# Four heads' last 64 queries in one block: joint remainder scoring in an attention and gated MLP kernel

## The chip, the cores and the metric

The kernel runs on one core of a Trainium2 chip. The core has a matrix engine (TensorE, PE in the profile), a vector engine (VectorE, DVE), a scalar engine (ScalarE, ACT), a general engine (GpSimd, POOL) and a queue engine (SyncE, SP) that issues nearly all transfers. The metric is the time of one execution in microseconds, the median of several runs. The profile describes one execution.

## The reference

Eight batches, eight heads, 576 positions, 64 values per head. Attention with a bias that depends on the position of the query and on the distance to the key, and then a gated layer: a causal convolution with five taps gives the gate, and one matrix product before and one after it mix the 512 channels.

```python
scores = scale * np.matmul(q, k.transpose(0, 1, 3, 2))
x = (psi_rel / psi_i)[..., None]            # log1p|i-j| / log1p(max(i,1))
bias = np.maximum(x @ w1 + b1, 0.0) @ w2    # one value per head
scores = scores + bias.transpose(2, 0, 1)[None, :, :, :]
attn = softmax(scores)                      # written out in the reference
x = matmul(attn, v), heads side by side     # (8, 576, 512)
gate = sigmoid(causal 5-tap convolution of x by conv_w)
out = (gate * (x @ w_val)) @ w_out
```

Everything is float32.

## The kernel before

**Pairs.** The work of attention is cut into 32 pairs of heads: `pair(n)` handles heads 2p and 2p+1 of batch b, where `order` lists the pairs so that two pairs with l = 0 and l = 1 of the same batch and the same half of the heads follow each other. One pair's queries and keys lie in one tile `qk`, head 0 on partitions 0 to 63 and head 1 on partitions 64 to 127, since a head has 64 values.

**Blocks.** The 576 queries of a head make four blocks of 128 (c = 0 to 3) and a remainder of 64 (c = 4, `NM`). For a main block `qkm` (L623) scores both heads with four matmuls: two halves of 288 keys for each head. The 64-row contractions of the two heads occupy different row halves of PE. Each f32 matmul shows as two records in the trace. For the remainder `qkr` (L635) the host has laid out the last 64 queries of both heads in one 128x128 stationary matrix and the keys of both heads in 640 columns with zeros between (`QW`, `RW`), so that two matmuls of 320 columns over all 128 rows give 64 rows of scores for each head. The part of the 640 columns that belongs to no key of the row is masked through the bias tile `biasr`, which holds -1e30 there.

**After the scores.** `logits` (L665, DVE) adds the bias and takes the maximum, `expo` (L677, ACT) exponentiates and sums. Then there are two ways, chosen for each pair in `TRANS`. A "T" pair is normalised in float32 (`norm`, L722, POOL or DVE), transposed on PE with an identity (`tp`, L762), copied out of PSUM (`tev`, ACT or DVE) and multiplied with V in float32. A "D" pair is split into two float16 halves (`top`, then `rest`, L252, mostly POOL), transposed by a DMA on SP's queue (`swap`, L796, for a main block and L799 for the remainder), and multiplied in three float16 products; the sums are divided out at the end through a small product with the identity (`rb`, L881; in the remainder L914) and a multiplication (`mu`, `mur`). `piece` (L832) is the product with V for two blocks at a time, in two column halves of PE, one per head; `rem_mm` (L904) is that of the remainder.

**The gated layer.** When all four pairs of a batch are done, `mlp` runs its convolution on DVE, and the products `val` (L1075) and `outp` (L1132) on PE. Before all attention, `bias_rows` builds the bias for all heads in DRAM (L365 on PE), from which `load_bias` fetches 128 queries of two heads at a time.

**Order.** `Plan` holds every step as a task with the engines that may run it, an estimated cost, its dependencies, a priority and the buffers that it takes. `Plan.order` walks through the tasks with a model of the engines, takes on each engine the ready task with the best priority, picks the engine for tasks that may run on several (weighted by `LOAD`), and thus writes out a fixed order for each engine; the chip then executes these queues in order. The priorities come from tables: `PAIR_AT` for each pair, `MLP_AT` for each batch, `OFFS` for each kind of step. `BUFS` gives the number of buffers in each ring, `RING` the ring that each kind of buffer uses, `LOOK` how far a ring may be taken out of order, and `MODES` the tiling of PE for each kind of step, whose change the model charges.

Of the kernel before, what the change touches and what calls it, by code (L numbers as in the profile page):

```python
# [32 lines left out]
NEG = -1.0e30  # L33
RW = S + REM
QW = (NM + 1) * P
# [6 lines left out]
MLP_AT = (27, 17, 14, 9, 8, 19, 12, 70)  # L42
PAIR_AT = (1, 3, -1, 0, -0.5, -1, 2.5, -2.5, -4.5, -5, -0.5, -0.5, -0.5, 0.5, 2.5, -1.5, -2, -2.5, -2, 1.5, 1.5, 1, -2.5, -0.5, -1.5, -5, -5.5, -7, 0, 3, 0.5, 0.5)
TRANS = tuple(x == "T" for x in "TTTDTTTTDTTDDTDDDDDTDDTDDDDDDDDD")
BUFS = dict(w=13, d=5, pt=2, sp=2, ps=4, qk=2, rel=4, be=6, xp=2, xh=1, gh=1, gx=1)
RING = dict(er="w", hlr="w", raw="w", e="d", hl="d", xo="w", vt="w", ptr="w", gate="w", gf="w", ot="w", tt="ps", po="ps", pm="ps", cv="ps")
LOOK = dict(w=14.02, ps=60.04, d=6.72, be=3.8, gh=227.3, pt=9.76, xh=21.35, sp=1.22, xp=0.44)
# [9 lines left out]
OFFS = dict(qkr=-5, ldx=3, swap=4.25, qk_ld=-1, qkm=-5, norm=4, piece=4, val=5.25, outp=7.75, mur=2.25, bias_store=-0.75, conv=-9.25, taps=-5.25, split_hi=-0.25, rb=-4.5, rest=-15.5, ldv=0.5, w_hi=-1, logits=1.75, relu=-3.25, ost=-1.25, bias_fin=0.25, ote=0.25, double_step=10.5, store=1, ghi=1.75, sig=-5.75, vtr=5, recip=-3, glo=-1, ev=3.25, tev=4, evr=1, w_sub=-7.5, gf=-3, w_ld=-5.25, mu=0, w_lo=7.5, bias_mm=0, bias_ld=0.75, expo=-2.25, prod=-1.25, vlo=1, cw=-3, vhi=5, eps=-0.25, vmax=-15.5, acc=0, split_lo=5.5, close_bias=2.5, rem_mm=4, top=-0.25, vinv=-0.25, tp=-3.25, vscale=-1.75, constant=4.75, constant_ev=-2)  # L57
# [147 lines left out]
def attention_gated_mlp(  # L205
# [23 lines left out]
    for k in set(BUFS) & {"sp", "ps", "w", "d", "pt", "qk"}:  # L229
        mem = dict(space=PSUM) if k in ("sp", "ps") else {}  # L230
        pools[k] = ctx.enter_context(tc.tile_pool(name="pool_" + k, bufs=1, **mem))
# [25 lines left out]
    biasr = [cp.tile([P, RW], F32, name=f"biasr_{l}") for l in range(2)]  # L257
# [55 lines left out]
    for t in biasr:  # L313
        G.memset(t[0:REM, S:RW], NEG)
        G.memset(t[REM:P, 0:REM], NEG)

# [113 lines left out]
    def load_bias(run, hg, l, c, pri):  # L430

        p = 2 * hg + l

        def bias_ld(e):
            if c < NM:
                SP.dma_start(biasm[l][c], bias_rows_of(c, 2 * p, 2))
            else:
                SP.dma_start(biasr[l][0:REM, 0:S], bias_rows_of(c, 2 * p, 1))
                SP.dma_start(biasr[l][REM:P, REM:RW], bias_rows_of(c, 2 * p + 1, 1))

        deps = stored[c] + users_of_bias.get((run - 1, l, c), [])
        return add([("S", 1.65 if c < NM else 0.9)], bias_ld, deps, pri)
# [87 lines left out]
    spilled, arrived, taker = {}, {}, {}  # L530

    def pair(n):
# [4 lines left out]
        tr = TRANS[n % len(TRANS)]  # L537
        pace = PACE[n] if n < len(PACE) else 2
        top_, bot = slice(0, D), slice(D, P)
# [3 lines left out]
        def qk_ld(e):  # L543
            SP.dma_start(new(qk, [P, QW + RW], F32), qkd[b, p])

        loaded = add([("S", 1.85)], qk_ld, (), s0 - 8, [qk])
# [59 lines left out]
        ptr = Buf("ptr")  # L606
        nms, rinvs, sm, invs, rsum = {}, {}, None, {}, {}
        es, exps, inv = {}, {}, {}
# [3 lines left out]
        for c in range(NM + 1):  # L612
            w = S if c < NM else RW
            sps = [Buf("sp") for _ in range(2 if c < NM else 1)]

            def qkm(e, c=c, sps=sps):
# [3 lines left out]
                for j in range(2):  # L620
                    for a, r in enumerate((top_, bot)):
                        x = QW + a * REM + j * hw
# [8 lines left out]
            def qkr(e, sps=sps):  # L631

                t, hw = new(sps[0], [P, 2, 512], F32), RW // 2
                for j in range(2):
                    T.matmul(  # L635
                        t[:, j, 0:hw],
                        lhsT=qk.t[:, NM * P : QW],
                        rhs=qk.t[:, QW + j * hw : QW + (j + 1) * hw],
                        start=True,
                        stop=True,  # L640
                    )

            qkt = add([("P", 1.17 if c < NM else 1.1)], qkm if c < NM else qkr, [loaded], s0 + pace * c, sps, [qk])
            for a in range(2 if c < NM else 1):
                h = s0 + pace * c + a
                sp = sps[a]
                if a == 0:
                    eb = Buf("e" if c < NM else "er")
                    es[c] = eb

                def part(c=c, a=a, w=w):
                    return es[c].t[:, a * S : a * S + w]

                def logits(e, c=c, a=a, w=w, sp=sp, part=part):
                    if a == 0:
                        new(es[c], [P, 2 * S if c < NM else RW], F32)
                    nonlocal sm
                    if a == 0:
                        nms[c] = smp.tile([P, 2], F32, name="nm", tag="nm", bufs=20)
# [4 lines left out]
                    bias = biasm[l][c][:, a, :] if c < NM else biasr[l]  # L664
                    V.tensor_tensor_reduce(  # L665
                        out=part().rearrange("p (j f) -> p j f", j=2),
                        in0=sp.t[:, :, 0 : w // 2],
# [8 lines left out]
                def expo(e, c=c, a=a, part=part):  # L676
                    A.activation(  # L677
                        out=part(),
                        in_=part(),
# [6 lines left out]
                def eps(e, c=c):  # L686

                    if tr:
                        rinvs[c] = smp.tile([P, 2], F32, name="rinv", tag="rinv", bufs=20)
                        o, u = rinvs[c], sums[c]  # L690
                        if c == NM:
                            o, u = o[:, 0:1], u[:, 0:1, :]
                    else:
                        x, w = (c // 2 * 4, 4) if c < NM else (8, 1)
# [11 lines left out]
                t1 = qkt  # L706
                bl = bias_task.get((run, l, c))
                if bl is None:
                    bl = bias_task[run, l, c] = load_bias(run, hg, l, c, h - 6)
                t2 = lg = add([("V", 0.68)], logits, [t1, bl, lg if a else None], h + 0.5, [eb] if a == 0 else (), [sp])  # L710
                users_of_bias.setdefault((run, l, c), []).append(t2)
                t3 = add([("A", 0.77)], expo, [t2], h + 1)
                exps[c, a] = t3
                if tr:
                    if c < NM and a == 0:
                        continue
                    tr_ = add([("V", 0.08)], eps, [exps[c, x] for x in range(a + 1)], h + 1.3)
                    tr_ = add([("V", 0.08)], recip, [tr_], h + 1.5)

                    def norm(e, a, c=c, w=w):  # L720
                        t = es[c].t[:, a * S : a * S + w]
# [9 lines left out]
                    for x in range(a + 1):  # L731
                        moved[c, x] = add([("G", 0.73), ("V", 0.43)], partial(norm, a=x), [tr_], h + 1 + x)
                else:
                    if a == 0:
                        hls[c] = Buf("hl" if c < NM else "hlr")
                    hl = hls[c]

                    def top(e, c=c, a=a, w=w, part=part, hl=hl):
                        if a == 0:
                            new(hl, [P, 2, RW] if c == NM else [P, 2, 2, S], F16)  # L740
                        copy(e, hl.t[:, 0, :] if c == NM else hl.t[:, 0, a, :], part())

                    def rest(e, c=c, a=a, part=part, hl=hl):
                        f = (lambda x: hl.t[:, x, :]) if c == NM else (lambda x: hl.t[:, x, a, :])
                        sub(e, f(1), part(), f(0))
# [4 lines left out]
                    if c == NM or (c % 2 and a):  # L750
                        g = c // 2
                        x = add([("V", 0.08)], eps, [exps[x] for x in exps if x[0] // 2 == g] + [rsum.get(g - 1)], h + 2)
                        rsum[g] = add([("V", 0.08)], recip, [x, rsum.get(g - 1)], h + 2.2)
            if tr:
                todo = []
                for k0, kn in ((0, 4), (4, 4), (8, 1)) if c < NM else ((0, 4), (4, 1)):
# [9 lines left out]
                    def tev(e, c=c, tt=tt, k0=k0, kn=kn):  # L766
                        if c == NM:
                            if k0 == 0:
                                new(ptr, [P, 5, P], F32)
# [7 lines left out]
                    d = [moved[c, 0]] + ([moved[c, 1]] if c < NM and k0 else [])  # L777
                    x = h + 2 + k0 / 4
                    t1 = add([("P", 0.112 * kn)], tp, d, x, [tt], [es[c]])
                    first = k0 == 0 and (c == NM or c % 2 == 0)  # L780
# [7 lines left out]
            else:  # L788
                first = c == NM or c % 2 == 0

                def swap(e, c=c, first=first):
                    hl = hls[c]
                    if c < NM:
                        if first:
                            new(halves[c // 2], [P, 2, 18, P], F16)
                        SP.dma_start_transpose(halves[c // 2].t[:, c % 2], hl.t.rearrange("p w a f -> p (w a f)"))  # L796
# [4 lines left out]
                d = [moved[c, a] for a in range(2 if c < NM else 1)]  # L801
# [3 lines left out]
                moved[c] = [add([("S", 2.95 if c < NM else 1.6)], swap, d, h + 2.5, tk, [hls[c]], 0.7)]  # L805


        prods = [(0, 0)] if tr else [(0, 0), (5, 0), (0, 9)]
        halfs = (slice(0, D), slice(D, P))
# [85 lines left out]
        por = Buf("tt")  # L895
        prods_r = [(0, 0)] if tr else [(0, 0), (5, 0), (0, 5)]

        def rem_mm(e):
            t = bank(por)
            k = 0  # L900
            for v0, w0 in prods_r:
                for x in range(5):
                    for r in halfs:
                        T.matmul(  # L904
                            t[r, 0:D],
# [328 lines left out]
```

## Time and profile before

| What | Value |
|---|---|
| Timed runs | 747.43, 747.57, 747.65 us; median 747.57 |
| Span of the profiled execution | 748.5 us, 0.9 above the median of the timed runs |
| PE busy | 704.3 us (94%) |
| DVE, ACT, POOL busy | 583.9 (78%), 575.0 (77%), 481.9 (64%) us |
| DMA, share of 16 engines' time | 83.6% on SP's queue |
| Granted PE clock, mean | 0.990 |

Busy time is the union of an engine's instructions. PE's matmuls overlap each other and their ends are modelled, so the distance between starts says more about a block than the length of its records. A DMA share above 1 means that packets' times overlap on an engine. Lines such as L635 are lines of the kernel before.

### The profile page before, as it was taken

Reading aid. Unit: us, or ns where it says so; the run is one execution under the profiler, and the core shown is the slowest. Engines: PE = TensorE matmul, PEld = TensorE weight load, DVE = VectorE, ACT = ScalarE, POOL = GpSimd, SP = SyncE. Lnnn points to the kernel's source line nnn. Section 1 sums busy time; section 2 is a strip of 40 time slices with the busy share of each in tenths; the row PEclk is TensorE's granted clock in tenths of the full one; section 3 lists DMA queues with packets and bytes.
Section 4 is the critical chain, followed back from the end, with each engine's and each line's share of the span. In section 5 each row is a group of like instructions: output and inputs, shape, how many; then the busy total and the mean of one; then the engine's idle time right before and its main releaser. Section 6 shows DMA issues by size and latency. Waiting matters only on the chain.

```text
span 748.5 us, 17263 instructions
## 1 busy us (share of the span) xinstructions
PE 704.3 (94%) x6122; PEld 498.4 (67%) x6122; DVE 583.9 (78%) x1590; ACT 575.0 (77%) x1277; POOL 481.9 (64%) x553
## 2 busy tenths in 40 slices
PE   5768999999989999999999999999999899999997
PEld 2214666666566666687687677767777678688886
DVE  6996698988879979988588768977579889897431
ACT  6988577777778997898677976797767988985632
POOL 1003369556767866699874695668787787876842
PEclk9989999999999999999999999999999999999999
DMA  8888248569893897899999689899999999996211
GB/s 274 280 267 270 80 151 190 146 193 281 170 228 104 145 201 185 177 199 211 224 212 212 140 184 231 259 247 194 235 221 194 226 247 208 198 170 133 71 48 51
DMA packets 273221, 143.23 MB, mean 191 GB/s; under 512 B 243312, under 2 KB 243568, under 8 KB 273136
## 3 DMA queue, kind: packets, MB, share of 16 engines
q1 hardware_dynamic: 272992, 141.84, 83.6%
q8 instruction: 48, 0.79, 0.4%
q10 hardware_dynamic: 144, 0.29, 0.2%
q14 instruction: 37, 0.30, 0.1%
HBM read 56.77 MB, written 25.05 MB: 109 GB/s over the span
## 4 chain that ended last, share of the span: by engine, by line
PE 57%; DMA 12%; DVE 12%; ACT 10%; issue 4%; POOL 3%; SPq 0%; POOLq 0%; ACTq 0%; DVEq 0%
PE t_sp L623 13%; PE t_ps L832 11%; PE t_ps L1132 11%; PE t_ps L1075 9%; DMA t_pt<-t_d 6%; PE t_ps L762 4%; PE t_sp L635 4%; DVE t_d L665 3%; DMA bias_d<-t_be 3%; DVE t_ps L1018 3%; ACT t_d L677 2%; PE t_ps L904 2%; DMA t_w<-vd 1%; PE t_ps L881 1%; DVE rel L346 1%
## 5 line engine op out<-in xcount | busy, mean ns | idle before, releaser
L677 ACT ACTIVATE t_d<-t_d,nm 128x576 f32<-128x576 f32 x256 | 197.8, 774 | 56.9 <-DVE nm L665 54.9
L252 POOL TENSOR_TENSOR t_d<-t_d 128x576 f16<-128x576 f32 x160 | 209.8, 1324 | 45.7 <-ACT t_d L245 37.6
L665 DVE CUSTOM_DVE_ANT_0 t_d<-t_sp,bias 128x576 f32<-128x576 f32 x256 | 188.2, 750 | 22.1 <-PE t_sp L623 10.4
L623 PE MATMUL t_sp<-t_qk 64*128 64x288 f32 x1024 | 174.7, 431 | 6.1 <-DVE nm L665 5.5
L832 PE MATMUL t_ps<-t_pt,t_w 128*64 128x256 f16 (+1 forms) x1680 | 141.7, 309 | 5.0 <-DMA t_pt<-t_d 3.7
L722 POOL TENSOR_SCALAR t_d<-t_d,rinv 128x576 f32<-128x576 f32 x96 | 72.8, 769 | 106.5 <-DVE rinv L704 58.6
L623 PEld LDWEIGHTS t_sp<-t_qk 64*128 64x128 f32 x1024 | 99.0, 186 | 55.1 <-issue 17.4
L1018 DVE SCALAR_TENSOR_TENSOR t_ps<-t_xp,convw,t_ps 128x288 f32<-128x288 f32 x168 | 86.9, 518 | 3.4 <-ACT t_ps L1009 0.8
L1075 PE MATMUL t_ps<-xh,wv 128*128 128x320 f32 (+1 forms) x512 | 83.4, 300 | 0.2 <-ACT t_pt L245 0.2
L245 ACT CAST t_d<-t_d 128x576 f16<-128x576 f32 x113 | 75.1, 669 | 6.6 <-POOL t_d L252 3.0
L832 PEld LDWEIGHTS <-t_w 128*64 128x64 f16 x1200 | 61.1, 109 | 25.0 <-issue 22.2
L1075 PEld LDWEIGHTS t_ps<-xh,wv 128*128 128x128 f32 x512 | 71.6, 188 | 8.5 <-issue 4.7
L1132 PE MATMUL t_ps<-wo,gh 128*128 128x512 f32 x256 | 71.0, 409 | 1.0 <-ACT gh L245 1.0
L762 PE MATMUL t_ps<-ident,t_d 128*128 128x128 f32 x432 | 62.7, 280 | 2.5 <-POOL t_d L722 0.9
L762 PEld LDWEIGHTS t_ps<-ident,t_d 128*128 128x128 f32 x432 | 47.0, 140 | 23.5 <-issue 8.3
L245 ACT COPY t_pt<-t_ps 128x512 f32<-128x512 f32 (+1 forms) x98 | 48.6, 516 | 11.4 <-PE t_ps L762 11.2
L1132 PEld LDWEIGHTS t_ps<-wo,gh 128*128 128x128 f32 x256 | 45.3, 188 | 16.2 <-issue 4.3
L365 PE MATMUL t_ps<-rel,w 128*32 128x288 f32 (+17 forms) x352 | 40.4, 525 | 14.6 <-ACT t_be L384 11.6
L1085 DVE TENSOR_TENSOR t_w<-t_ps,t_w 128x256 f32<-128x256 f32 (+1 forms) x64 | 28.5, 452 | 30.7 <-PE t_ps L1075 28.2
L252 POOL TENSOR_TENSOR gl<-t_w,gh 128x256 fp32r<-128x256 f32 x52 | 39.6, 762 | 19.4 <-ACT gh L245 15.8
L245 ACT COPY t_w<-t_ps 128x512 f32<-128x512 f32 (+2 forms) x64 | 31.8, 503 | 22.0 <-PE t_ps L1132 20.7
L677 ACT ACTIVATION_READ_ACCUMULATOR t_d<-t_d,nm 128x1 f32 x256 | 48.6, 190 | 0.0
(115 smaller groups left out, 1167.5 us busy)
## 6 DMA issues: line engine op xcount, KB each, us to landing
t_qk<-qkd SPq DMA_DIRECT2D x32, 640.0 KB, 4.7
bias<-bias_d SPq DMA_DIRECT2D x24, 576.0 KB, 4.8
bias_d<-t_be SPq DMA_DIRECT2D x36, 295.5 KB, 4.6
out<-t_w SPq DMA_DIRECT2D x32, 256.0 KB, 2.6
t_w<-vd SPq DMA_DIRECT2D x20, 320.0 KB, 3.9
xs<-t_w SPq DMA_DIRECT2D x16, 288.0 KB, 3.4
t_xp<-xs SPq DMA_DIRECT2D x8, 576.0 KB, 4.6
t_w<-vn SPq DMA_DIRECT2D x12, 320.0 KB, 5.2
```

What stands on the lines that cost most here:

```text
L245: A.copy(out=out, in_=in_)
L252: (V if e == "V" else G).tensor_tensor(out=out, in0=in0, in1=in1, op=ALU.subtract)
L365: T.matmul(pb[32 * g : 32 * g + 32, 0 : y - x], lhsT=w28, rhs=rel[g].t[:, x:y], start=True, stop=True, tile_position=(0, 32 * g),)
L623: T.matmul(ts[a][:, j, 0:hw], lhsT=qk.t[r, c * P : (c + 1) * P], rhs=qk.t[r, x : x + hw], start=True, stop=True,)
L665: V.tensor_tensor_reduce(out=part().rearrange("p (j f) -> p j f", j=2), in0=sp.t[:, :, 0 : w // 2], in1=bias.rearrange("p (j f) -> p j f", ...
L677: A.activation(out=part(), in_=part(), func=AF.Exp, bias=nms[c][:, a : a + 1], scale=-1.0, accum_out=sums[c][:, a, 0:1],)
L722: (G if e == "G" else V).tensor_scalar(out=t, in0=t, scalar1=rinvs[c][:, a : a + 1], scalar2=1.0, op0=ALU.mult, op1=ALU.mult,)
L762: T.transpose(t[:, k * P : (k + 1) * P], es[c].t[:, (k0 + k) * P : (k0 + k + 1) * P], ident)
L832: T.matmul(po.t[r, 0:256], lhsT=vt.t[:, v0 + t, r], rhs=pt[:, w, :, :] if tr else pt[:, :, w, :], start=(k == 0), stop=(k == 5 * len(prods ...
L1018: V.scalar_tensor_tensor(out=o, in0=x, scalar=cw, in1=t, op0=ALU.mult, op1=ALU.add)
L1075: T.matmul(pm.t[:, 0:w], lhsT=pools["wv"][wi][:, k, d * P : (d + 1) * P], rhs=xb.t[xi][:, k, 0:w], start=(q == 0 and k == 0), stop=(q == 2 ...
L1132: T.matmul(pm.t, lhsT=gb.t[gi][:, k, o : o + P] if o < 256 else gx.t[gi][:, k, :], rhs=pools["wo"][wi][:, k, :], start=(q == 0 and k == 0) ...
```

## The change

The remainders of the two pairs of a batch (l = 0 and l = 1) are scored together. The pair with l = 0 has only its four main blocks; the pair with l = 1 has a fifth block that holds 64 queries of each of the four heads: head a of both pairs in PSUM tile a, the first pair on partitions 0 to 63, the second on 64 to 127. Eight matmuls with 64x64 tiles and 288 keys each fill it. It then goes the way of any main block, with two logits, two exponentials and so on, and a transposition of 2 x 2 x 576 float16 values, or nine transposes on PE. `finish` then multiplies the remainder with V once per pair. The zero padding of `qk` and of the remainder's bias, and the masks, are gone. Since the two pairs share a block, `TRANS` is now given per couple (ten pairs on PE's path instead of twelve). Tables of priorities, buffers and load weights have new values.

```diff
-MLP_AT = (27, 17, 14, 9, 8, 19, 12, 70)
+MLP_AT = (25, 17, 12, 18, 4, 14, 12, 51)
-TRANS = tuple(x == "T" for x in "TTTDTTTTDTTDDTDDDDDTDDTDDDDDDDDD")
-BUFS = dict(w=13, d=5, pt=2, sp=2, ps=4, qk=2, rel=4, be=6, xp=2, xh=1, gh=1, gx=1)
-RING = dict(er="w", hlr="w", raw="w", e="d", hl="d", xo="w", vt="w", ptr="w", ...)
+TRANS = tuple(x == "T" for x in "TTDTTDDDDDDTDDDD")
+BUFS = dict(w=11, d=6, pt=2, sp=2, ps=4, qk=3, rel=4, be=6, xp=2, xh=1, gh=1, gx=1)
+RING = dict(raw="w", e="d", hl="d", xo="w", vt="w", ptr="d", ...)
-MODES = dict(qkm=1, piece=2, rem_mm=2, rb=2, bias_mm=3)
+MODES = dict(qkm=1, qkr=4, piece=2, rem_mm=2, rb=2, bias_mm=3)
-LOAD = dict(P=1.27, V=1.2, A=0.36, G=0.47, S=0.27)
+LOAD = dict(P=0.665, V=1.2, A=0.486, G=0.423, S=2.056)
...
-    biasr = [cp.tile([P, RW], F32, name=f"biasr_{l}") for l in range(2)]
+    biasr = cp.tile([P, 2, S], F32, name="biasr")
...
-                SP.dma_start(biasr[l][0:REM, 0:S], bias_rows_of(c, 2 * p, 1))
-                SP.dma_start(biasr[l][REM:P, REM:RW], bias_rows_of(c, 2 * p + 1, 1))
+                for x in range(2):
+                    SP.dma_start(biasr[x * REM : (x + 1) * REM], bias_rows_of(c, 4 * hg + 2 * x, 2))
...
-        tr = TRANS[n % len(TRANS)]
+        tr = TRANS[n // 2]
...
-            SP.dma_start(new(qk, [P, QW + RW], F32), qkd[b, p])
+            SP.dma_start(new(qk, [P, 2 * S], F32), qkd[b, p])
...
+        mine = mates[n] = dict(qk=qk, loaded=loaded, vt=vt, tv=tv)
+        both = [mates[n - 1], mine] if l else None
...
             def qkr(e, sps=sps):
-                t, hw = new(sps[0], [P, 2, 512], F32), RW // 2
+                ts, hw = [new(sp, [P, 2, 512], F32) for sp in sps], S // 2
                 for j in range(2):
-                    T.matmul(
-                        t[:, j, 0:hw],
-                        lhsT=qk.t[:, NM * P : QW],
-                        rhs=qk.t[:, QW + j * hw : QW + (j + 1) * hw],
-                        start=True,
-                        stop=True,
-                    )
+                    for a, r in enumerate(halfs):
+                        for m, o in zip(both, halfs):
+                            q = m["qk"].t
+                            x = S + j * hw
+                            T.matmul(
+                                ts[a][o, j, 0:hw],
+                                lhsT=q[r, NM * P : S],
+                                rhs=q[r, x : x + hw],
+                                start=True,
+                                stop=True,
+                            )
...
-                        new(ptr, [P, 10, P], F16)
-                        SP.dma_start_transpose(ptr.t, hl.t.rearrange("p w f -> p (w f)"))
+                        new(ptr, [P, 18, P], F16)
+                        SP.dma_start_transpose(ptr.t, hl)
...
+        for c in range(NM + 1 if l else NM):
+            block(c)
...
+        def finish(x1, o, me, ready, rsum_):
+            por = Buf("tt")
...
+                            T.matmul(
+                                t[r, 0:D],
+                                lhsT=vt.t[:, v0 + x, r],
+                                rhs=ptr.t[:, w0 + 4 * a + x, o],
...
+        if l:
+            for m, o in zip(both, halfs):
+                finish(m["x1"], o, m, moved[NM], rsum.get(2))
...
-    qk = np.zeros((B, NP, P, QW + RW), f32)
...
+    qk = np.concatenate([q.reshape(B, NP, P, S), k.reshape(B, NP, P, S)], axis=3)
```

`PAIR_AT`, `LOOK` and `OFFS` have new values throughout; in `OFFS` many steps of DVE, ACT and POOL now have large negative offsets (`expo` from -2.25 to -81.5, `ev` from 3.25 to -62), while `qkm` stays at -5 and `qkr` goes from -5 to -3.75.

More of the change, by code (lines that the diff above doesn't have):

```diff
@@ L611, in pair, with part, block @@
         hls = {}
-        for c in range(NM + 1):
-            w = S if c < NM else RW
-            sps = [Buf("sp") for _ in range(2 if c < NM else 1)]
+        mine = mates[n] = dict(qk=qk, loaded=loaded, vt=vt, tv=tv)
+        both = [mates[n - 1], mine] if l else None
+        ptr = Buf("ptr")
+        def part(c, a):
+            return es[c].t[:, a * S : (a + 1) * S]
+        def block(c):
+            nonlocal sm
+            exps = {}
+            sps = [Buf("sp") for _ in range(2)]
             def qkm(e, c=c, sps=sps):
@@ L729, in norm @@
                         )
[L731 removed]
+                    for x in range(2):
                         moved[c, x] = add([("G", 0.73), ("V", 0.43)], partial(norm, a=x), [tr_], h + 1 + x)
@@ L749, in pair @@
                     moved[c, a] = t5
-                    if c == NM or (c % 2 and a):
+                    if a and (c == NM or c % 2):
                         g = c // 2
-                        x = add([("V", 0.08)], eps, [exps[x] for x in exps if x[0] // 2 == g] + [rsum.get(g - 1)], h + 2)
+                        x = add([("V", 0.08)], eps, [every[x] for x in every if x[0] // 2 == g] + [rsum.get(g - 1)], h + 2)
                         rsum[g] = add([("V", 0.08)], recip, [x, rsum.get(g - 1)], h + 2.2)
@@ L755, in pair @@
                 todo = []
-                for k0, kn in ((0, 4), (4, 4), (8, 1)) if c < NM else ((0, 4), (4, 1)):
+                for k0, kn in (0, 4), (4, 4), (8, 1):
                     tt = Buf("tt")
@@ L768, in tev @@
                             if k0 == 0:
-                                new(ptr, [P, 5, P], F32)
+                                new(ptr, [P, 9, P], F32)
                             t = ptr.t[:, k0 : k0 + kn, :]
@@ L894, in pair @@
             x1 = add([("V", 0.34)], mu, [x0, x], d + 2, (), [po])
[L895 to L905, printed above, removed]
-                            lhsT=vt.t[:, v0 + x, r],
-                            rhs=ptr.t[:, w0 + x, r],
-                            start=(k == 0),
-                            stop=(k == 5 * len(prods_r) - 1),
-                        )
-                    k += 1
-            if not tr:
-                for r in halfs:
-                    T.matmul(
-                        t[r, D:P], lhsT=rinvs[NM][:, 0:1].to_broadcast([P, D]), rhs=ident[:, r], start=True, stop=True
-                    )
@@ L919, in evr @@
             if tr:
-                copy("V", xo_(512, S), por.t[:, 0:D])
+                t2 = add([("V", 0.14)], evr, [t1, x1], d + 0.5, (), [por])
             else:
-                A.activation(out=xo_(512, S), in_=por.t[:, 0:D], func=AF.Copy, scale=sc["t"][:, 1:2])
-        def mur(e):
-            V.tensor_tensor(out=xo_(512, S), in0=xo_(512, S), in1=por.t[:, D:P], op=ALU.mult)
-        def store(e):
-            SP.dma_start(xs[b][p], xo.t)
-        d = s0 + 13 + (pace - 2) * 4
-        dd = moved[NM] + [tv, x1] + ([] if tr else [rsum[2]])
```

166 lines of the change are left out of this document (89 added, 77 removed).

## The prediction, made before the result was known

> **What bounds the kernel now.** I read the head of the page first, then busy time by stage, then who waited for whom, then single blocks on PE.
>
> ```profile
> span 748.5 us, 17263 instructions
> PE 704.3 (94%) x6122; PEld 498.4 (67%) x6122; DVE 583.9 (78%) x1590; ACT 575.0 (77%) x1277; POOL 481.9 (64%) x553
> q1 hardware_dynamic: 272992, 141.84, 83.6%
> ```
>
> The profiled span is 748.5 us; the timed runs have a median of 747.57, so I take 0.9 off any span. PE is idle for 748.5 - 704.3 = 44.2 us in all. The windows view shows where (columns: stretch, length, busy us of PE, PEld, DVE, ACT, POOL, then clock, DMA share, GB/s):
>
> ```profile
> 0.00:75.00 75.00, 53.17 (x432) 19.33 (x434) 60.26 (x154) 61.77 (x131) 9.53 (x36) 0.93 0.85 272
> 75.00:275.00 200.00, 194.54 (x1657) 129.99 (x1655) 166.65 (x503) 157.05 (x367) 131.75 (x141) 0.99 0.70 171
> 275.00:475.00 200.00, 196.45 (x1776) 144.17 (x1775) 162.03 (x446) 159.17 (x356) 145.90 (x165) 1.00 0.97 202
> 475.00:675.00 200.00, 193.23 (x1810) 147.15 (x1809) 165.65 (x444) 164.91 (x358) 155.42 (x161) 1.00 1.07 214
> 675.00:748.50 73.50, 66.90 (x455) 57.78 (x453) 29.27 (x46) 32.09 (x69) 39.33 (x53) 0.99 0.26 72
> ```
>
> Half of the idle time, 21.8 us, lies in the first 75 us, where the bias is built. Over the 600 us of attention PE stands idle 15.8 us (2.6%), and no other engine is above 84% there. PE sets the pace, so work taken from PE should come off the time almost whole. The second resource to watch is DMA: its share rises from 0.70 to 1.07 as the pairs turned by DMA transpose come to dominate. The waits view says that PE hardly ever stands for it (us, times, longest):
>
> ```profile
> PE t_ps L365 <- ACT t_be L384: 11.6, 15, 1.9
> PE t_sp L623 <- DVE nm L665: 5.5, 8, 1.3
> PE t_ps L832 <- DMA t_pt<-t_d: 3.7, 8, 0.8
> ```
>
> **The change, term 1: the joint remainder block.** Now every pair of heads scores its last 64 queries in one 128x128 block with K=128, zeros and 640 key columns (L635); a main block scores two heads in two 64x128 tiles (L623). On the timeline of PE, a block's real price is the distance from its start to the next start (the second column includes the drain):
>
> ```profile
> 555.96 1.24 PE L623 MATMUL t_sp<-t_qk 64*128 64x288 f32 x8
> 557.13 1.17 PE L832 MATMUL t_ps<-t_pt,t_w 128*64 128x256 f16 x18
> 558.23 1.34 PE L635 MATMUL t_sp<-t_qk 128*128 128x320 f32 x4
> 559.51 0.85 PE L832 MATMUL t_ps<-t_pt,t_w 128*64 128x256 f16 x12
> ```
>
> A main block costs 1.17 us, a remainder block 1.28. The joint block issues 16 records (8 matmuls, each in two passes as the x8 for four matmuls shows) on four 64x64 tiles, with 288 columns. No row here has four tiles. If all four run at once it is a main block: 1.17 us. If only two do it is two main blocks: 2.34. That both row halves (L623) and column halves (L832, 128*64) run beside each other is shown by the groups below. All four one after another would undo both, so I leave that out. I take 1.20, near the lower end, since each split is shown alone at full effect. 32 x 1.28 = 41.0 becomes 16 x 1.20 = 19.2: **21.8 us off PE** (3.5 at the other end).
>
> Weight loads are the one thing that could break it: two tiles share a row half. In the column-split groups two tiles share all rows (busy us, mean ns | idle):
>
> ```profile
> L832 PE MATMUL t_ps<-t_pt,t_w 128*64 128x256 f32 x480 | 63.9, 395 | 0.0
> L832 PEld LDWEIGHTS t_ps<-t_pt,t_w 128*64 128x64 f32 x480 | 30.9, 138 | 26.6 <-issue 11.8 <-ACT t_pt L245 1.3 <-ACT t_d L677 0.8
> ```
>
> 480 matmuls of 256 columns in 63.9 us are 0.52 ns per column and record; 1.17 us for 8 records of 288 is 0.51. Loads of 138 ns each hide just as well where tiles share rows. The Trainium skill (TensorE: Matmul & The Clock Gate, Part 3) says that a weight load overlaps matmuls in flight only when its row group differs. This trace does not bear that out; by that rule each joint block would also show a load per round, as in rival B.
>
> **Term 2: two pairs fewer on the PE path.** A "T" pair normalises on POOL, transposes on PE and multiplies in f32; a "D" pair splits into f16 halves, transposes by DMA and uses three f16 products. There are 12 T pairs of 32 now and 10 after (five couples). Prices from the timeline, again start to start:
>
> ```profile
> 545.86 0.66 PE L904 MATMUL t_ps<-t_w 128*64 128x64 f16 x30
> 546.33 0.34 PE L914 MATMUL t_ps<-ident,rinvs 128*64 128x64 f32 x4
> 546.59 0.86 PE L1075 MATMUL t_ps<-xl,wv 128*128 128x320 f32 x4
> ...
> 549.53 1.83 PE L832 MATMUL t_ps<-t_pt,t_w 128*64 128x256 f16 x30 [0.32 <-DMA t_pt<-t_d]
> 551.19 0.60 PE L881 MATMUL t_ps<-ident,rinvs 128*64 128x128 f32 x8
> 551.72 1.31 PE L623 MATMUL t_sp<-t_qk 64*128 64x288 f32 x8
> ```
>
> A D pair: 2 x 1.66 (products) + 2 x 0.53 (L881) + 0.47 + 0.26 (remainder) = 5.1 us. For a T pair the chain of waits gives merged pieces (start, us):
>
> ```profile
> 92.12 0.73 PE t_ps L904 x20
> ...
> 94.12 1.45 PE t_ps L832 x12
> ...
> 100.10 1.24 PE t_ps L762 x10
> ```
>
> 40 records at 1.45/12 = 4.8, 41 transposes at 0.124 = 5.1, remainder 0.73: 10.6 us. Two pairs moved save 2 x 5.5 = **11.0 us** of PE. The joint block has 9 transposes where two T pairs had 10: 5 x 0.124 = **0.6 us**. Together 33.4 us of PE's 704.3.
>
> **What the others get.** POOL gains two pairs of L252 subtractions and loses two of L722:
>
> ```profile
> L252 POOL TENSOR_TENSOR t_d<-t_d 128x576 f16<-128x576 f32 x160 | 209.8, 1324 | 45.7 <-ACT t_d L245 37.6 <-DVE rinvs L701 1.9 <-PE t_sp L623 1.8
> L722 POOL TENSOR_SCALAR t_d<-t_d,rinv 128x576 f32<-128x576 f32 x96 | 72.8, 769 | 106.5 <-DVE rinv L704 58.6 <-ACT t_pt L245 12.4 <-ACT t_d L677 6.7
> L665 DVE CUSTOM_DVE_ANT_0 t_d<-t_sp,bias 128x576 f32<-128x576 f32 x256 | 188.2, 750 | 22.1 <-PE t_sp L623 10.4 <-POOL t_d L252 4.6 <-DMA bias<-bias_d 2.6
> L677 ACT ACTIVATE t_w<-t_w,nm 128x640 f32<-128x640 f32 x32 | 26.4, 825 | 10.3 <-DVE nm L665 10.2
> L677 ACT ACTIVATE t_d<-t_d,nm 128x576 f32<-128x576 f32 x256 | 197.8, 774 | 56.9 <-DVE nm L665 54.9
> ```
>
> 2 x 8 x (1.32 - 0.77) = +8.8 us on POOL, some 69% of a 716 us span. The joint block still has two logits and two exponentials per couple, each of 576 columns instead of 640: 32 x 51 ns = 1.6 us off ACT, much the same off DVE; all of it off the path. The planner's load weights also push a few casts from ACT (0.36 to 0.486) to DVE and POOL, which have room.
>
> DMA issues (size, us to landing):
>
> ```profile
> t_pt<-t_d SPq DMA_TRANSPOSE x80, 5.3
> ...
> t_w<-t_w SPq DMA_TRANSPOSE x40, 4.0
> ```
>
> Transposes, in columns of 128 halves: now 80 x 2304 + 40 x 1280 = 235,520; after, 22 pairs x 4 plus 11 joint ones make 99 x 2304 + 22 x 1280 = 256,256, or 8.8% more. They are between 42% of the traffic (128 rows of 2 bytes a column, of 141.84 MB) and all of it, so +23 to +55 us of the 626 us (83.6%) of DMA time; the 32 qk loads fall from 1,280 to 1,152 columns, 2.1 MB less in all, about -9. That makes 640 to 672 us over 716: 89 to 94% on average, under the 1.07 shown above, and these windows show that PE can be full at more (same columns):
>
> ```profile
> 575.00:600.00 25.00, 22.27 (x237) 16.79 (x232) 22.41 (x63) 23.82 (x50) 17.99 (x19) 1.00 1.13 228
> 600.00:625.00 25.00, 25.00 (x221) 20.04 (x220) 22.05 (x61) 20.52 (x50) 21.41 (x23) 1.00 1.12 238
> ```
>
> So I cost DMA at nothing, covered by PE's own work; without the cover it is rival C.
>
> **Term 3: buffers and order.** Queries and keys of the first pair, its V and its output tile are now held until the joint block of the second; qk goes from 2 to 3 buffers, d from 5 to 6 (e, hl and now ptr), w from 13 to 11 while three short users leave it. DVE now waits 4.6 us in all for a d buffer (its row above, behind L252), so I add nothing. The order of everything is new and cannot be read from the diff. Its bounds: at best all 44.2 us idle on PE go; at worst the whole 600 us look like the worst window above, 2.73 of 25 idle, 65 us instead of 15.8, or +50. The old order is within 2.6% of full in the middle, so I take zero gain there, and let a tenth of the PE saving be lost to waits that become visible: 30 of 33.4 us. Sum: 748.5 - 30 - 0.9 = **717.6, say 718 us**.
>
> **Rivals.**
> - *B, the four tiles don't do what they say.* Two at a time: 41.0 - 16 x 2.34 = 3.5 saved there, with 11.6 from term 2 that is 15.1, nine tenths of it 13.6: 734 us. Speaks for it: no four-tile row here. Against: each split alone runs at full rate. The milder form, four exposed loads of 138 ns per joint block, costs 16 x 0.55 = 8.8 us: 727.
> - *C, DMA paces the D stretches.* Couples 5 to 10 are D without a break, 12 pairs. If PE's saving in D pairs (11 joint blocks x 1.36 = 15 us) is eaten by DMA that is already at 1.07, 33.4 - 15 = 18.4 remain, 17 after waits: 731. For: the share climbs with D pairs. Against: PE waits 3.7 us for transposes.
> - *D, slower: the joint block as a barrier.* The remainder of both pairs now ends behind one block: two logits, exponentials, casts, a POOL subtraction of 1.32 us, a transposition of 5.3 us and only then two remainder products and two outputs, while V, output and qk buffers of both pairs stay taken. SP issues in order, and its head already waits 77.5 us on L252:
>
> ```profile
> SPq L796 <- POOL t_d L252: 77.5, 25, 5.9
> ```
>
>  A late joint transposition holds back the next pair's loads. If PE then stands 3 us at each of the 16 joints: 747.6 - 33.4 + 48 = 762. It decides from 33.4/16 = 2.1 us a joint. Against: main blocks of the next pair can be issued in front, and the order knows the buffers.
>
> **How the numbers follow.** Forecast 0.66 (its own range 712 to 726), B 0.15 (two at a time 0.11, exposed loads by the skill's rule 0.04), C 0.09, D 0.07, a wash 0.03. The low end is the full 33.4 us and 8 us, about a third, of the start-up idle (pair 0 no longer waits for the last bias rows): 706; the high end takes in B and C with some waits: 740. Outside lie D and little else. A difference under 0.2% is no change for this kernel: faster 0.89, same 0.03, slower 0.08.
>
> **What would show it.** Term 1: the joint block's 16 records and the next start 1.2 us later (2.3 means B). Term 2: about 405 transposes on PE and 22 D pairs; PE busy near 671 us. C: PE waiting for t_pt transposes by tens of us with the share above 1.1. D: PE idle before the remainder products, over 2 us a couple. Wrong outright if PE's idle time in the middle rises from 15.8 to over 45 us.

## The result

| | Before | After |
|---|---|---|
| Median of 8 runs | 747.50 us | 743.05 us |
| Range of these runs | 746.0 to 749.0 | 739.7 to 745.9 |
| Ratio to before | | 0.9948, 95% interval 0.9923 to 0.9973 |
| Span of the profiled execution | 748.5 us | 738.3 us |

The change makes the kernel about 4 us faster, 0.5%. The prediction was 718 us with a range of 706 to 740. The profiled execution of the changed kernel is one of its fastest (its own time is 740.2), so its span flatters the change by some 3 us. A time is about 1.8 us longer than the span of its execution (740.16 and 738.3); by that the profiled execution before, 748.5, was about 3 us slower than its median. So the two spans differ by 10.2 us where the medians differ by 4.5.

The head of the page and the stages (columns as in the prediction: stretch, length, busy us of PE, PEld, DVE, ACT, POOL, clock, DMA share, GB/s), after:

```profile
span 738.3 us, 17494 instructions
PE 682.8 (92%) x6263; PEld 489.5 (66%) x6263; DVE 581.6 (79%) x1541; ACT 574.6 (78%) x1266; POOL 495.7 (67%) x572
q1 hardware_dynamic: 293664, 145.05, 85.9%
```

```profile
0.00:75.00 75.00, 52.87 (x456) 21.00 (x457) 61.53 (x159) 60.83 (x130) 9.02 (x32) 0.98 0.84 273
75.00:275.00 200.00, 185.88 (x1639) 123.33 (x1639) 169.19 (x495) 159.58 (x363) 134.63 (x138) 0.96 0.71 180
275.00:475.00 200.00, 190.49 (x1885) 145.24 (x1885) 155.22 (x411) 159.31 (x358) 159.23 (x171) 0.97 1.09 216
475.00:675.00 200.00, 196.15 (x1871) 150.52 (x1871) 171.34 (x439) 166.35 (x360) 152.02 (x178) 1.00 0.98 209
```

PE is busy for 21.5 us less (704.3 to 682.8) and idle for 11.3 us more (44.2 to 55.5). From 75 to 475 us it now stands idle 23.6 of 400 us, where it stood 9.0, and its granted clock there is 0.96 and 0.97 instead of 0.99 and 1.00. The waits say on what (us, times, longest):

```profile
PE t_sp L625 <- DVE nm L671: 14.2, 17, 2.8
...
PE t_sp L641 <- DVE nm L671: 3.0, 3, 1.1
PE t_ps L837 <- DMA t_pt<-t_d: 2.3, 4, 1.2
```

L625 is the main block's scoring, L641 the joint block's, L671 the logits. PE waits for the logits to free a score tile in PSUM: 17.2 us in all, where it was 8.6 (L623 and L635 before). It hardly waits for transposes (2.3 us before L837).

What the change itself does came out nearly as priced. On PE's timeline an undisturbed joint block (16 records, four tiles) is followed by the next step 97.92 - 96.78 = 1.14 us later, and the group of all joint blocks has 24.0 us where L635 had 42.7. First the block, then the groups after, then the two score groups before:

```profile
96.78 1.20 PE L641 MATMUL t_sp<-t_qk 64*64 64x288 f32 x16
97.92 0.66 PE L765 MATMUL t_ps<-ident,t_d 128*128 128x128 f32 x4
```

```profile
L625 PE MATMUL t_sp<-t_qk 64*128 64x288 f32 x1024 | 185.4, 440 | 14.4 <-DVE nm L671 14.2
...
L765 PE MATMUL t_ps<-ident,t_d 128*128 128x128 f32 x405 | 57.8, 281 | 2.5 <-ACT t_pt L243 0.8 <-DVE rinv L705 0.4 <-POOL t_d L250 0.3
...
L641 PE MATMUL t_sp<-t_qk 64*64 64x288 f32 x256 | 24.0, 442 | 3.0 <-DVE nm L671 3.0
```

```profile
L623 PE MATMUL t_sp<-t_qk 64*128 64x288 f32 x1024 | 174.7, 431 | 6.1 <-DVE nm L665 5.5 <-DMA t_qk<-qkd 0.2
...
L635 PE MATMUL t_sp<-t_qk 128*128 128x320 f32 x128 | 42.7, 457 | 3.1 <-DVE nm L665 3.1
```

405 transposes are as forecast. But the 1024 records of the main blocks, untouched by the change, take 185.4 us instead of 174.7. The steps that the change makes cheaper give up 35 us by the busy times of their groups (18.7 in the remainders, 16.6 in the products, transposes and divisions of the two pairs moved); 10.7 us, nearly a third, is spent again in score blocks that run at a lower clock or are interrupted. One stretch shows how. Around the gates of a batch, ACT is full and PE starves:

```profile
250.00:275.00 25.00, 18.27 (x136) 11.27 (x137) 17.00 (x50) 23.36 (x47) 16.64 (x16) 0.82 0.86 180
```

```profile
260.81 1.28 ACT L1046 ACT_TABLE_LOAD   x1
262.10 2.40 ACT L1046 ACTIVATE t_w<-t_w 128x576 f32<-128x576 f32 x4
264.52 1.28 ACT L683 ACT_TABLE_LOAD   x1
```

```profile
259.24 2.18 PE L641 MATMUL t_sp<-t_qk 64*64 64x288 f32 x12 [0.96 <-DVE nm L671]
261.46 3.12 PE L625 MATMUL t_sp<-t_qk 64*128 64x288 f32 x8
264.51 2.46 PE L837 MATMUL t_ps<-t_pt,t_w 128*64 128x256 f16 x30
```

The eight records at 261.46 take 264.51 - 261.46 = 3.05 us, with a granted clock of 0.50 in that time; with the full clock they take 1.17 (the main block in the prediction).

A full ACT alone does not do this. The kernel before has a gate in the same 25 us (its table load starts at 265.30), with ACT as full, and PE is not starved there:

```profile
250.00:275.00 25.00, 24.21 (x217) 17.05 (x216) 20.38 (x58) 23.81 (x49) 15.96 (x14) 1.00 1.01 194
```

The lower mean clock is made of a few spells. In the changed kernel the granted clock is 0.57, 0.60, 0.51, 0.57 and 0.57 in the windows 139 to 143, 150 to 154, 259 to 266, 272 to 280 and 347 to 355 us, 31 us in all. From 75 to 675 us the clock held back, added up, is 13.6 us of full speed, where in the kernel before it is 1.6. Each spell comes right behind 4 us in which PE was busy for 2.3 to 2.9 us. Such a pause is not enough for it, though: before the change PE was busy for 2.4 of 4 us from 515 us on, and the clock stayed at 1.00 from 515 to 523 us.

### The profile page after: what moved, and what is told of

The parts are those of the page before. It is cut to its first block, busy times and chain, and to the rows that moved or that the text cites. A ratio compares the mean times of both kernels' runs of the same rounds, so it can differ in the third digit from the quotient of the medians.

```text
span 738.3 us, 17494 instructions
## 1 busy us (share of the span) xinstructions
PE 682.8 (92%) x6263; PEld 489.5 (66%) x6263; DVE 581.6 (79%) x1541; ACT 574.6 (78%) x1266; POOL 495.7 (67%) x572
## 3 DMA queue, kind: packets, MB, share of 16 engines
q1 hardware_dynamic: 293664, 145.05, 85.9%
## 4 chain that ended last, share of the span: by engine, by line
PE 31%; DVE 15%; ACT 13%; POOL 6%; issue 6%; DMA 6%; SPq 0%; POOLq 0%; DVEq 0%; ACTq 0%
PE t_sp L625 8%; PE t_ps L1148 7%; PE t_ps L837 6%; PE t_ps L1091 6%; DVE t_d L671 5%; ACT t_d L683 5%; DVE t_ps L1034 4%; POOL t_d L250 3%; DMA t_d<-t_d 3%; ACT t_d L243 2%; ACT t_w L1046 2%; PE t_ps L765 1%; PE t_ps L911 1%; ACT L1046 1%; PE t_ps L886 1%
## 5 line engine op out<-in xcount | busy, mean ns | idle before, releaser
L250 POOL TENSOR_TENSOR t_d<-t_d 128x576 f16<-128x576 f32 x198 | 259.3, 1324 | 42.9 <-ACT t_d L243 31.7
L683 ACT ACTIVATE t_d<-t_d,nm 128x576 f32<-128x576 f32 x288 | 222.2, 772 | 69.4 <-DVE nm L671 66.3
L671 DVE CUSTOM_DVE_ANT_0 t_d<-t_sp,bias 128x576 f32<-128x576 f32 x256 | 187.7, 750 | 34.9 <-PE t_sp L625 13.6
L625 PE MATMUL t_sp<-t_qk 64*128 64x288 f32 x1024 | 185.4, 440 | 14.4 <-DVE nm L671 14.2
L625 PEld LDWEIGHTS t_sp<-t_qk 64*128 64x128 f32 x1024 | 103.6, 190 | 67.9 <-DVE nm L671 34.1
L837 PE MATMUL t_ps<-t_pt,t_w 128*64 128x256 f16 (+1 forms) x1720 | 137.6, 308 | 5.3 <-DMA t_pt<-t_d 2.3
L243 ACT CAST t_d<-t_d 128x576 f16<-128x576 f32 x152 | 99.7, 667 | 4.3 <-POOL t_d L250 1.6
L837 PEld LDWEIGHTS <-t_w 128*64 128x64 f16 x1320 | 71.5, 114 | 25.1 <-issue 17.5
L765 PE MATMUL t_ps<-ident,t_d 128*128 128x128 f32 x405 | 57.8, 281 | 2.5 <-ACT t_pt L243 0.8
L247 POOL TENSOR_SCALAR t_d<-t_d 128x576 f16<-128x576 f32 x46 | 32.3, 703 | 34.6 <-ACT t_d L683 24.0
L683 ACT ACTIVATION_READ_ACCUMULATOR t_d<-t_d,nm 128x1 f32 x288 | 54.4, 189 | 0.0
L359 PE MATMUL t_ps<-rel,w 128*32 128x288 f32 (+17 forms) x352 | 37.8, 508 | 15.4 <-ACT t_be L378 10.2
L243 ACT COPY t_pt<-t_ps 128x512 f32<-128x512 f32 (+1 forms) x81 | 38.4, 498 | 11.0 <-PE t_ps L765 10.2
L1091 PE MATMUL t_ps<-xl,wv 128*128 128x256 f32 (+1 forms) x256 | 45.5, 298 | 0.0
```

The costliest lines, as they stand in the source:

```text
L243: A.copy(out=out, in_=in_)
L250: (V if e == "V" else G).tensor_tensor(out=out, in0=in0, in1=in1, op=ALU.subtract)
L359: T.matmul(pb[32 * g : 32 * g + 32, 0 : y - x], lhsT=w28, rhs=rel[g].t[:, x:y], start=True, stop=True, tile_position=(0, 32 * g),)
L625: T.matmul(ts[a][:, j, 0:hw], lhsT=qk.t[r, c * P : (c + 1) * P], rhs=qk.t[r, x : x + hw], start=True, stop=True,)
L671: V.tensor_tensor_reduce(out=part(c, a).rearrange("p (j f) -> p j f", j=2), in0=sp.t[:, :, 0 : S // 2], in1=bias.rearrange("p (j f) -> p j ...
L683: A.activation(out=part(c, a), in_=part(c, a), func=AF.Exp, bias=nms[c][:, a : a + 1], scale=-1.0, accum_out=sums[c][:, a, 0:1],)
```

## The experiments

All of them keep the order of the kernel that they are made from: the planner's costs, tables and queues are untouched, only the instructions of some steps are made cheaper or dearer. So they ask what a microsecond of each engine is worth where it stands. Times below are ratios to the kernel before, and, worked out from them with 747.5 us, the difference to the kernel that was edited (the changed kernel at 0.9948 is -3.9 us). Each ratio is known to between 0.2% and 0.7%, 1.5 to 5 us (the 95% interval in brackets), and a difference of two of them less well.

**Theories.** 1: PE sets the pace (the prediction's). 2: no engine sets it alone; a fixed order couples all. 3: DMA paces the D stretches. 4: the low PE clock gives the saving back. 5: PE was half of what sets the pace before the change. In its first form, theory 2 names the chain from the scores through DVE and ACT.

### Less work on PE alone

```diff
 def qkm(e, c=c, sps=sps):
+    # block c = 3 only (b_pe_all: every main block): upper halves of the words, one pass
+    q_, k_ = (y.bitcast(bfloat16).rearrange("p (n t) -> p n t", t=2)[:, :, 1] for y in (q_, k_))
```

> The kernel before, its order unchanged; the main block c = 3 of every pair is scored from the upper halves of the f32 words (bfloat16, one pass) on PE, so about 0.8 us less PE work in each of 32 blocks, 25 us in all, about what the change takes from PE. The computation loses precision there and nothing else. Theory 1 (the prediction's: PE sets the pace, what is taken from PE comes off nine tenths): about -22 us, ratio 0.970. Theory 2 (PE only looked like the bound; at a fixed order the score-to-softmax chain through DVE and ACT sets the pace almost as often): less than half, -4 to -10 us, ratio 0.987 to 0.995.

Measured: 743.58 us, ratio 0.9931 (0.9901 to 0.9960): -5.2 us. PE's busy time falls by 24.8 us; four fifths of that does not reach the time.

```profile
PE 679.5 (92%) x5994; PEld 478.8 (65%) x5994; DVE 589.7 (80%) x1590; ACT 574.3 (78%) x1277; POOL 482.6 (65%) x553
```

> The changed kernel with the same cut: block c = 3 of every pair scored from bfloat16 halves, 25 us less PE work, order unchanged. Theory 1 (PE still paces, the change's loss is in its order): about -20 us against the changed kernel, so near 723 us, ratio 0.967 to before. Theory 2 (PE no longer paces): -10 us or less, 733 us or more.

Measured: 748.63 us, ratio 1.0016 (0.9980 to 1.0052): +5.1 us against the changed kernel, with PE busy for 18.1 us less (682.8 to 664.7). Less work made it no faster, perhaps slower.

> The kernel before, order unchanged, every main block scored from bfloat16 halves: about 100 us less PE work. Theory 2: the floor that the other engines and the order set is already reached with 25 us less (743.6), so 735 to 744. Theory 5 (PE was still half of the chain): 720 or less.

Measured: 735.97 us, ratio 0.9827 (0.9777 to 0.9876): -12.9 us, where the main score blocks take 101 us less (174.7 to 73.7) and PE is busy for 78.9 us less in all. This is the run that settles the main reading. The page and the stages of this kernel:

```profile
PE 625.4 (85%) x5610; PEld 427.6 (58%) x5610; DVE 582.8 (79%) x1590; ACT 574.6 (78%) x1277; POOL 484.2 (66%) x553
```

```profile
75.00:275.00 200.00, 168.29 (x1553) 106.40 (x1552) 177.45 (x537) 166.49 (x389) 143.84 (x153) 0.99 0.73 182
275.00:475.00 200.00, 178.60 (x1656) 126.33 (x1656) 164.14 (x448) 161.51 (x359) 148.03 (x169) 0.98 0.96 206
475.00:675.00 200.00, 172.40 (x1695) 132.17 (x1695) 163.89 (x429) 161.16 (x348) 153.09 (x159) 0.97 1.04 209
```

PE is idle 80.7 of these 600 us instead of 15.8, and the time moves by 12.9. The chain of waits had already turned with 25 us less. Shares of the span, the kernel before and then b_pe:

```profile
PE 57%; DMA 12%; DVE 12%; ACT 10%; issue 4%; POOL 3%; SPq 0%; POOLq 0%; ACTq 0%; DVEq 0%
```

```profile
PE 45%; DVE 23%; ACT 13%; DMA 8%; issue 6%; POOL 4%; SPq 0%; DVEq 0%; ACTq 0%; POOLq 0%
```

### More work on PE

```diff
 def qkm / qkr (changed kernel; qkm in the kernel before)
-    for j in range(2):
+    for j in (0, 1, 0, 1):      # a_more, b_more: block c = 3; a_rem2: the joint block
```

> The changed kernel, order unchanged; the main block c = 3 of every pair is scored twice over, so 8 more records of about 0.97 us in each of 32 blocks, 31 us more PE work. Theory 1 (PE paces): +28 us, 771. Theory 2 (no single engine paces a fixed order): +5 to +15 us. Theory 4 (PE's granted clock falls where PE waits, and that gives back what is saved): the clock rises from 0.978 towards 0.99 and the time stays within 6 us of 743.

Measured: 765.47 us, ratio 1.0255 (1.0200 to 1.0309): +22.9 us.

> The kernel before with the same 31 us of PE work added. Theory 1: +28 us, 775. Theory 2: +5 to +15 us, since PE stood nearer to the pace there than in the changed kernel; more than in a_more. Theory 4: within 6 us, like a_more.

Measured: 768.98 us, ratio 1.0262 (1.0219 to 1.0306): +19.6 us. PE's busy time went from 704.3 to 732.2.

> The changed kernel, order unchanged; each joint remainder block is scored twice over, 16 records more, about 1.0 us in each of 16 blocks, 16 us in all, so that the joint blocks cost PE nearly what the 32 remainder blocks of the kernel before cost. It gives back by itself what four 64x64 tiles at once save. Theory 1: +14 us, 757. Theory 2: the four tiles' saving is worth less than 6 us at this order: 743 to 749.

Measured: 754.43 us, ratio 1.0087 (1.0059 to 1.0115): +10.4 us. PE's busy time went from 682.8 to 694.3.

All three lie between the forecasts of theories 1 and 2, so neither had the size of this side. Adding and taking away are not alike. By PE's busy time, a microsecond added costs 0.7 to 0.9 (PE is busy for 28.8 us more in a_more), and one taken away brings about 0.2 in the kernel before and nothing in the changed one. The reading that fits both sides is that PE ends neck and neck with the rest: more work makes it last, less work leaves the others last.

Theory 4 in the form forecast here falls too: with 31 us more PE work the clock of the changed kernel was 0.973 in the profile, not higher than 0.978. But where PE work was taken away, the clock did fall. The mean over the runs is 0.992 for the kernel before, 0.985 in b_pe and 0.973 in b_pe_all; it is 0.978 for the changed kernel and 0.963 in a_pe. So some of what was taken away may have been given back through the clock; no run separates that. It is not the whole, since PE stood idle for 80.7 us in b_pe_all.

And a_rem2 splits the result: with joint blocks that cost PE nearly what the old remainders cost (38.1 us against 42.7), the new order takes 0.87% longer than the old one. The four tiles are worth about 10 us in it; the rest of the edit (the order, two more D pairs, the buffers, not told apart here) costs about 6.5.

### Less work on one of the others

```diff
 a_dve:  -partial(taps, tps=(1, 2))        +partial(taps, tps=(1,))
 a_act:  expo() without accum_out; the sums are a constant 1.0
 a_dma, b_dma: for c >= 2 swap() transposes the high half only; piece() uses it as the low half too
 a_pool: for c >= 2 rest() is tensor_scalar(part, 2**-12), not part - high half
```

> The changed kernel; one of the five convolution taps is left out for all batches but the last (56 DVE instructions of 0.52 us, 29 us of DVE's 582). Theory 1: no change, within 3 us of 743. Theory 2 (the logits are late because DVE and ACT are full): -8 to -15 us, 728 to 735.

Measured: 739.75 us, ratio 0.9892 (0.9827 to 0.9956): -4.2 us, not clear of nothing.

> The changed kernel; the exponential no longer writes its row sum (the sums are a constant, so the normalisation is left out), which takes 288 accumulator reads from ACT, about 0.1 us of queue time each, 29 us, perhaps 54. Theory 1: within 3 us of 743. Theory 2: ACT's exponentials release d buffers and sums earlier: -8 to -20 us.

Measured: 745.26 us, ratio 0.9955 (0.9922 to 0.9987): +0.5 us, with 23 us less busy on ACT. Theory 2 in its first form wanted 8 us or more from each of these two runs and is not borne out.

> The changed kernel; for the blocks c = 2 and 3 of D pairs only the high float16 half is transposed by DMA, and the third product uses it again in place of the low half (precision is lost, the count of matmuls is the same): 44 transpositions of 2304 columns become 1152, 50,688 of 256,256 columns less, a fifth. If DMA paces the D stretches (theory 3): -15 us or more, 728 or less. If no single resource paces a fixed order (theory 2): within 6 us of 743.

Measured: 737.46 us, ratio 0.9888 (0.9855 to 0.9921): -4.5 us. DMA's share fell from 85.9% to 76.0%.

> The kernel before with the same edit: 40 transpositions halved, 46,080 of 235,520 columns less. Theory 3: -15 us or more, 733 or less. Theory 2: within 6 us of 747.9.

Measured: 742.52 us, ratio 0.9942 (0.9921 to 0.9962): -4.3 us.

> The changed kernel; in blocks c = 2 and 3 of D pairs the low float16 half is a scaled copy (one input, about 0.7 us) in place of the subtraction (1.32 us), so the low half is wrong: 88 POOL instructions, about 55 us less on POOL. If POOL is what the transposes wait for (the queue of SP waits 134 us on it): -10 to -20 us. Theory 2: within 6 us of 743.

Measured: 736.79 us, ratio 0.9866 (0.9837 to 0.9895): -6.1 us for 68 us less busy on POOL. The edit takes in the joint block as well (c = 4), so 110 instructions are cheaper and not 88. DVE is busy for 15.8 us less too (581.6 to 565.8) with the same 1541 instructions: 17 of its subtractions for `xl` take 11.0 us instead of 17.7. So this run relieved two engines.

None of these reliefs gave more than 6.1 us. Theory 3 falls: a tenth of the DMA share is worth 4 us. POOL's was the largest; SP's queue does wait for POOL's subtractions (134.0 us at L799, before 77.5 at L796):

```profile
SPq L799 <- POOL t_d L250: 134.0, 48, 6.7
```

### Several at once

These put together the cuts above: a_all and b_all have those on PE (c = 3), DVE, POOL and DMA, a_npe has them without PE's, a_all_act has ACT's as well.

> The changed kernel with four cuts at once: PE (bfloat16 scores in c = 3, 25 us), DVE (one tap, 29 us), POOL (55 us), DMA (a fifth of the transposed columns). Theory 2 (the engines are coupled by a fixed order and few buffers, so that each one's relief is lost at the next one's wait, but the relief of all is not): more than the sum of the single effects, -25 us or more, 718 or less. If a common cause outside these four sets the time (ACT, or the clock of PE): within 10 us of 743.

Measured: 721.05 us, ratio 0.9656 (0.9630 to 0.9682): -21.8 us, where the single effects add up to 5.1 - 4.2 - 6.1 - 4.5 = -9.7. That is short of the 25 that theory 2 named, and more than the sum by 12 us, where the intervals of all these ratios together leave an uncertainty of some 9 us (an estimate).

> The changed kernel with the cuts on DVE, POOL and DMA but none on PE. Theory 2 (PE and the others are equally near to the end of the chain): with the others relieved PE paces, so this lands well above the 721 of all four cuts, 731 to 736, and the 25 us of PE work are worth 10 to 15 us there, where they were worth nothing alone. If PE's share is nothing: 721.

Measured: 727.61 us, ratio 0.9704 (0.9652 to 0.9757): -18.2 us against singles of -14.8. That is below the 731 to 736 expected. Against a_all, PE's 25 us are worth 3.6 us by the ratios here, 6.6 by the medians, less than the 10 to 15 expected. The intervals of the two ratios overlap, but the four runs of each do not (720.6 to 722.5 and 725.1 to 729.2 us), so PE's cut probably counts here, where alone it cost 5.

> The kernel before with four cuts at once, as in the changed kernel: PE 25 us, one convolution tap 29 us of DVE, POOL's subtraction replaced in c = 2 and 3 (50 us), a fifth of the transposed columns. If the old order is coupled like the new one: about -20 us, 727; the single cuts on PE and DMA gave -4 each. If the old order was PE-bound after all with DMA beside it: about the sum, 738.

Measured: 730.11 us, ratio 0.9750 (0.9702 to 0.9798): -18.7 us, nearer to the first forecast. It is not shown that the whole is more than its parts here: the cuts on DVE and POOL were not timed alone in this order, and with their sizes from the changed kernel the sum is -5.2 - 4.3 - 4.2 - 6.1 = -19.8.

> The changed kernel with the four cuts and the accumulator reads of ACT left out as well (about 29 us of ACT; alone it gave nothing). Theory 2: ACT is the one left at the end of the chain, so now it is worth 8 to 20 us: 701 to 713. If ACT is not in the chain: 721.

Measured: 716.13 us, ratio 0.9555 (0.9503 to 0.9607): -29.4 us, so ACT's relief, worth nothing alone, brings 7.6 by the ratios and 4.9 by the medians, just short of the 8 to 20 expected.

Theory 2 stands in this form for the changed kernel: the reliefs of DVE, POOL and DMA about add up, that of ACT counts only when the others have theirs, and that of PE probably so. It was not shown which link (the two score tiles, the d buffers, the fixed queues) ties them; that would need other orders.

### The gate without a table change

This computes everything. The gate as (1 + tanh(x/2))/2 needs no other activation table than the exponential, and the factor 1/2 goes into the last copy, so ACT's table loads around each gate go.

```diff
-A.activation(out=gates[k].t, in_=gates[k].t, func=AF.Sigmoid)
+A.activation(out=gates[k].t, in_=gates[k].t, func=AF.Tanh, scale=0.5)
 def gf: -V.tensor_tensor(pm * gate)   +V.scalar_tensor_tensor((gate + 1.0) * pm)
 def ote: -copy(e, ot.t, pm.t)         +the same copy with a factor 0.5
```

> The changed kernel, order unchanged, whole computation: the gate is computed as (1 + tanh(x/2)) with the final 0.5 folded into the copy of the output, so that no activation table has to be loaded between exponential and gate (in the kernel before 7 + 6 loads of 1.28 us, 16.7 us of ACT, always just ahead of and behind the gates), if tanh and the exponential share a table. If the stretches where ACT is full at a gate (250 to 275 us: ACT 23.4 of 25, PE clock 0.82) are what the new order lost: -6 to -15 us against the changed kernel, 728 to 737. If single reliefs are lost whatever their place: within 4 us of 743.

Measured: 739.63 us, ratio 0.9905 (0.9868 to 0.9942): -3.2 us against the changed kernel, not clear of nothing.

> The kernel before with the same gate. If the gates' place matters in both orders: -4 to -12 us, less than in the changed kernel, whose PE has more room. If single reliefs are lost whatever their place: within 4 us of 747.

Measured: 741.32 us, ratio 0.9910 (0.9879 to 0.9941): -6.7 us against the kernel before, where less than in the changed kernel was expected. ACT's table loads are down from 14 to one, of 1.3 us, and ACT's busy time from 575.0 to 558.5:

```profile
PE 698.0 (94%) x6122; PEld 496.4 (67%) x6122; DVE 582.8 (79%) x1590; ACT 558.5 (75%) x1264; POOL 482.5 (65%) x553
```

It is the only relief of ACT that showed by itself, and only in the old order (where leaving out the row sums was not tried). In the changed kernel the starved stretch got a little better (250 to 275 us, PE 19.79 busy instead of 18.27, clock 0.86 instead of 0.82), so the table loads are at most a part of what is lost there:

```profile
250.00:275.00 25.00, 19.79 (x151) 13.08 (x150) 17.48 (x49) 20.07 (x43) 16.64 (x16) 0.86 0.91 190
```

Both kernels with this gate are faster than the kernel before; a_tanh and b_tanh can't be told apart. The changed kernel with it has the lower median, 739.63.

## Why the prediction was wrong

- **Term 1, the joint block: right in its mechanism, a little large in its size.** 1.14 us start to start against 1.20. Four 64x64 tiles do run at once, rival B falls, and so does its milder form: the block at 96.78 us has 16 records in 1.14 us, which leaves no room for four weight loads of 138 ns beside 1.17. The Trainium skill (TensorE: Matmul & The Clock Gate, Part 3) has a weight load overlap matmuls in flight only when its row group differs; this trace does not agree with it. The group as a whole saved 18.7 us and not 21.8: the 16 joint blocks average 1.50 us (24.0/16), since some fell into waits and low clock.
- **Term 2, two pairs moved: right in its counts** (405 transposes; 22 D pairs), and worth 16.6 us by the groups' busy times against the 11.6 priced. The two terms together are 35.3 us against 33.4. PE's busy time was to be near 671 us and is 682.8, since the main score blocks got 10.7 us slower as above.
- **The step that failed stands in the first part: "PE sets the pace, so work taken from PE should come off the time almost whole."** That was false of the kernel before, at its own order and without any change: 25 us less gave 5.2, about 100 us less gave 12.9. The tenth taken off for waits should have been some eight tenths, and the order should have cost some 6.5 us on top. I read it from PE being busy 94% and idle 15.8 of 600 us. Both are true and neither says that the others would be done any earlier. What the profile's page did show was four engines at 64 to 94% in an order fixed for each, where a share of idle time on one says only that it is rarely kept waiting now.
- The Trainium skill (Perfetto Trace Analysis, Identifying the Most-Contended Engine) says that the busy share of matmuls is a poor measure of how close TensorE is to its limit, because they are pipelined, and that the share of weight loads is one of two better ones. By that share PE (PEld 67%) stood behind DVE (78%) and ACT (77%) before the change, which speaks against my reading. No run here shows that it measures better: in b_pe_all both fall by nine points, from 94% to 85% and from 67% to 58%.
- **DMA and POOL "at nothing": wrong in kind, small in size.** Their reliefs bring 4 to 6 us, so their work was not wholly covered by PE. Rival C had PE's saving eaten by DMA alone; a fifth of the transposed columns is worth only 4.5 us.
- **Order "zero": wrong.** By a_rem2 everything but the four tiles costs about 6.5 us, although two more D pairs are in it, which take work off PE. PE's idle time from 75 to 675 us is 27.5 us, under the 45 that I named as the sign of an outright failure, and yet the gain was gone: the sign was set too high, because the saving also went into slower score blocks.
- **Rival D, the joint block as a barrier: not seen.** PE waits 3.0 us before L641 in all and 3.7 us before the remainder products (L911), 0.2 a couple, and none of its waits for transposes is above 2.3 us in total. The waits grew before the main blocks instead.
- The rivals shared the mistake. Each named one mechanism that would take the gain away; none was that the gain had not been there to take. The wash had a chance of 0.03 and no mechanism, and that is the case with which the chances (0.89 for faster, most of it for 30 us) should have begun.

Left open: why 25 us less on PE made the changed kernel slower by 5 us (the two intervals are only just apart, and the clock was lower), and how much of the loss is the clock and how much the waits. An estimate of the clock's part from the windows above: 13.6 - 1.6 = 12 us of PE time at most, if every microsecond of clock held back were one of time.

## What to carry to other kernels

A busy share near 100% on one engine does not make it the bound of a kernel with a fixed, balanced order: the engines can end together, as here, and then the worth of a saving has to be measured. Cut the engine's work in the old kernel, at its own order and with precision left out if need be, and time that; here one such run, b_pe, needs nothing of the change and shows the small worth. And price a change's order apart from its work: with the order kept, doubling the cheapened step again shows what the step is worth.

## What was unexpected in the hardware

- Sixteen records on four 64x64 tiles take 1.14 us, no longer than eight on two 64x128 tiles (1.17 us), with weight loads for every record.
- A score block after waits took 3.05 us instead of 1.17, with a granted clock of 0.50. None of PE's waits for the logits in this kernel was longer than 2.8 us.
- Cheaper instructions on POOL made DVE's shorter: 17 subtractions of DVE took 11.0 us instead of 17.7 in a_pool. What ties the two is not shown.
- tanh and the exponential need no table load between them: all but one of the loads of 1.28 us were gone. The Trainium skill (ScalarE: Activation LUTs, Table sets: the hidden batching unit) says so, and this trace agrees.
